# Chunk attention, then a top-1 cosine router with eight experts: two first weight loads issued from GpSimd, and three sums of the second stream computed by GpSimd

## The chip, the core and the metric

The kernel runs on one core of one Trainium2 chip. The metric is the device time of one execution in microseconds; the time of a kernel is the median of its runs. The profile shows one execution, with times counted from the start of its span. The engines are PE (TensorE: matmuls; "PEld" is its weight load), DVE (VectorE), ACT (ScalarE), POOL (GpSimd) and SP (SyncE, which here only issues DMAs). "SPq" and "POOLq" are the sequencers of SP and POOL, that is, their queues of instructions.

## The reference, cut to what matters

```python
# attention in chunks of 64: q, k, v are (8, 8, 576, 64)
scores = scale * (q_c @ k_c^T); attn = softmax(scores); out = attn @ v_c
x = out as (4608, 512)                                  # B*S rows, H*D columns
# router: one expert of 8 for each row
logits = normalise(x) @ normalise(expert_emb).T / tau
expert_idx = argmax(logits); gate_w = softmax(logits)[expert_idx]
for e in range(8):                                      # w1[e]: 512x1024, w2[e]: 1024x512
    h = maximum(x[mask_e] @ w1[e], 0)
    out[mask_e] = gate_w[mask_e] * (h @ w2[e])
```

Everything is float32. Which rows go to which expert is known only at run time.

## The kernel before, in words

**Two phases.** The first phase (to about 175 us of the span) computes the attention in 36 tiles of 128 rows, and the logits. It scatters each row into a DRAM buffer `spots`, where the rows of one expert lie together, in groups of 64 (`G`). At its end VectorE works out which group is computed in which step: `src_row` (where a group's rows lie), `eblk` (its expert), `fresh` and `swap` (whether other weights are needed than before), `after` and `more_e` (the next expert, and whether there is one). These are small integer tiles; the queues read them into registers.

The second phase is a row of steps. Each step `j` computes 128 rows: a group of 64 of stream 0, which walks up from expert 0, and a group of 64 of stream 1, which walks down from expert 7. So two sets of weights are in use at any time, `w1_sb[s]` and `w2_sb[s][buf]`, `s` = 0 or 1, each tile 2 MB. In the profile all of `w1_sb` and `w2_sb` read as `w`, and `next_w1` reads as `next_w`.

**What a step does.** `hidden_fast` (L323) computes `relu(x @ w1)` by Strassen's scheme in the form of Winograd: seven products of half the size instead of eight. Their order on PE is p1 (block B11 of w1), p2 (B21), p3 (B22), p5 (T1), p6 (T2), p7 (T3), p4 (T4). T1 to T4 are differences of blocks of w1. T1, T2 and T4 lie in `sums_sb[s]`; T3 overwrites B12 in w1 itself. Each product goes over both streams. `add_up` (L278, the instruction on L286) forms T1 to T4 by subtractions of 128x1024 elements on VectorE. `add_x` (L313) forms the sums S of the input, `turn_xb` (L198) turns the input's blocks. `result(j)` (L400) is the product with w2 (L408), scaling by the gate on ACT (L420) into the one buffer `y`, and a scatter to the output issued by POOL (L427). `y` has one buffer, so L420 of the next step waits until the scatter has read it.

Steps 0, 1 and 2 are computed without Strassen (`hidden_part`, L232); 0 and 1 still inside the first phase. The first Strassen step is step 3. Before it, VectorE must have formed T1, T2, T4 and T3 of both streams from the first weights (experts 0 and 7). The loop (L1146) writes, for `j` = 0: `add_up` of stream 0 between two pieces of the gates, then `result(0)`; for `j` = 1: `turn_next` (turn the input of step 3, issue the load of step 6, `add_x`), `add_up` of stream 1, the hidden part of step 2, and behind each of its halves T3 of that stream; then `result(1)`; from `j` = 2 on: `hidden_fast(j + 1)`, `result(j)`.

**Where the loads stand.** All loads of weights go through SP's queue (`load_when`, L169), in program order with the loads of rows (`load_x`, L158: four transfers `xin` on L148 and two `spot` on L154). A weight load is issued with a condition: its transfer takes place only where the flag is 1, but the instructions are always there: read the expert and the flag into registers (L132), then the DMA (L172). Ahead of the loop stand `load_x(4)`, `load_x(5)` and `load_w2(LONE)`, with `LONE` = 5: the second buffers of w2, first used by step 5, always loaded. In the loop, after `result(j)`, come `load_w2(next_of(j))` where that is 4 or more, and `load_behind(n)` (n = j + 2), which loads the next expert's w1 into `next_w1[s]`: `load_behind(3)` at j = 1 always loads, the later ones only where the expert before has been taken over. `load_w2(4)` stands after `result(3)`; it writes the buffers that results 0 to 4 read, and its flag is 0 where step 4 uses the same experts.

The order on each queue is the order of the program (a manual schedule); an engine waits at an instruction until the semaphores of what it needs have come. Where the expert changes, `take_next` (L290) copies three blocks by POOL (L296) while VectorE forms the sums.

Of the kernel before, what the change touches and what calls it, by code (L numbers as in the profile page):

```python
# [16 lines left out]
ENG = mybir.EngineType  # L17
# [8 lines left out]
def kernel(  # L26
# [11 lines left out]
    nc = tc.nc  # L38
    B, H, S, Dh = q.shape
    E, D = moe_expert_emb.shape  # L40
# [13 lines left out]
    NE = 4  # L54
# [6 lines left out]
    LONE = NE + 1  # L61

    def buf_of(j):
        return 0 if j < LONE else (j - LONE + 1) % 2
# [29 lines left out]
    w2_sb = [[keep.tile([P, KF, D], FP32, name=f"w2_{s}0")] for s in range(2)]  # L94
# [4 lines left out]
    w1_rows = moe_w1.rearrange("e (p c) f -> p e (c f)", c=KD)  # L99
    w2_rows = moe_w2.rearrange("e (p c) d -> p e (c d)", c=KF)  # L100
# [3 lines left out]
    eblk = keep.tile([P, NST], I32, name="eblk")  # L104
    fresh = keep.tile([P, NST], I32, name="fresh")
# [3 lines left out]
    after = keep.tile([P, NSW], I32, name="after")  # L109
    more_e = keep.tile([P, NSW], I32, name="more_e")  # L110

    def of_step(s, j):
        c = NST - 1 - (j - NE)
        return slice(G * s, G * s + 1), slice(c, c + 1)
# [6 lines left out]
    def whole(w):  # L121
        return w.rearrange("p c f -> p (c f)").unsqueeze(1)
# [8 lines left out]
    def number(ap, top, *engines):  # L131
        return nc.values_load(  # L132
            ap,
            engines=engines,
            min_val=0,
            max_val=top,
            skip_runtime_bounds_check_because="a count of comparisons, less than this",
        )
# [27 lines left out]
        r0 = (0, E - 1)[s] * R + G * j  # L166
        return spots[r0 : r0 + G * n, :]

    def load_when(w, rows, e, f):  # L169

        e, f = number(e, E - 1, ENG.SP), number(f, 1, ENG.SP)
        nc.sync.dma_start(  # L172
            out=whole(w), in_=rows[:, ds(e, 1), :], cond=f > 0, max_dma_last_dim=4096
        )

    def load_w2(j):
        for s in range(2):
            at = of_step(s, j)
            load_when(w2_sb[s][buf_of(j)], w2_rows, eblk[at], fresh[at])

    def load_behind(j):

        c = LEAST - 2 - j
        for s in range(2):
            at = (slice(G * s, G * s + 1), slice(c, c + 1))
            load_when(next_w1[s], w1_rows, after[at], more_e[at])

    def load_late(j):
        for s in range(2 if j != LEAST else 1):
# [79 lines left out]
    TS = ("T1", "T2", "T4")  # L269

    def block(s, m, w1=None):

        if m in TS:
            return sums_sb[s][:, TS.index(m)]
        u, v = UV[m]
        return (w1 or w1_sb)[s].rearrange("p (u c) (v x) -> p u v c x", u=2, v=2)[:, u, v]

    def add_up(s, w1, which):  # L278
        for o, a, b in (
            ("T1", "B12", "B11"),  # L280
            ("T2", "B22", "T1"),
            ("T3", "B22", "B12"),
            ("T4", "T2", "B21"),
        ):
            if o in which:
                nc.vector.tensor_tensor(  # L286
                    block(s, o), block(s, a, w1), block(s, b, w1), ALU.subtract
                )

# [155 lines left out]
    with (  # L445
# [43 lines left out]
        at = one.tile([P, 1], FP32, name="at")  # L489
# [551 lines left out]
        w = 2  # L1041
        for t in range(-1, 30):
            n = 2 if t in (8, 10, 24, 25) else 1
# [76 lines left out]
    next_w1 = [late_p.tile([P, KD, F], FP32, name=f"next_w1_{s}") for s in range(2)]  # L1120
    sums_sb = [late_p.tile([P, 3, KD // 2, F // 2], FP32, name=f"sums_{s}") for s in range(2)]

    load_x(NE)
    load_x(NE + 1)
    load_w2(LONE)

    with (
        tc.tile_pool(name="ps_h", bufs=1, space=PSUM, reuse_waits="tile") as ps_h,
        tc.tile_pool(name="ps_y", bufs=2, space=PSUM, reuse_waits="tile") as ps_y,
    ):  # L1130
        H_PS = [P, G // Q, KF * Q]

        def hidden_plain(j, w1, behind_it=None):
            for s in range(2 if j != LEAST else 1):
                ps = bank(ps_h, H_PS)
                for b in range(G // Q):
                    hidden_part(j, s, b, w1, None, None, ps)
                if behind_it is not None:
                    behind_it(s)

        def first_parts():
            for g in first_gates:
                next(g, None)

        first_parts()
        for j in range(LEAST - 1):  # L1146
            n = j + 2

            def turn_next():
                if n < LEAST:  # L1150
                    turn_xb(n)
                    if n + XBUF < NJ:
                        load_x(n + XBUF)
                    add_x(n)

            def swap_next():
                if NE <= n < LEAST:
                    take_next(n)

            if j == 0:  # L1160
                first_parts()
                add_up(0, None, TS)
                first_parts()
            elif j == 1:
                turn_next()
                add_up(1, None, TS)
                hidden_plain(2, w1_sb, lambda s: add_up(s, None, ("T3",)))
            else:
                gate = gate_parts(n) if n < LEAST else iter(())
                hidden_fast(j + 1, ps_h, gate, turn_next, swap_next)  # L1170

            result(j, ps_y)
            if NE <= next_of(j) < NJ:
                load_w2(next_of(j))
            if NE - 1 <= n < LEAST - 1:
                load_behind(n)
            elif n == LEAST - 1:
                load_late(LEAST)

        steps = number(n_steps, NST, ENG.PE, ENG.DVE, ENG.Activation, ENG.Pool, ENG.SP)  # L1180

        odd_one = number(n_odd, 1, ENG.PE, ENG.DVE, ENG.Activation, ENG.Pool, ENG.SP)

        def before_last():
            result(LEAST - 1, ps_y)
            load_w2(LEAST + 1)

        def step_alone(j, between=None):
            turn_xb(j)
            if j + XBUF < NJ:  # L1190
                load_x(j + XBUF)
            gates(j)
            hidden_plain(j, next_w1)
            if j + 1 < NJ:
                load_late(j + 1)
            if between is not None:
                between()
            result(j, ps_y)
            if j + 2 < NJ:
                load_w2(j + 2)  # L1200

        def more(j):
            if j == NJ:
                return

            with tc.If(steps > j - NE - 1):  # L1206
                step_alone(j)
                more(j + 1)

        had, had_mo, had_gate = dict(xin), dict(mo), dict(gate_of)  # L1210
        with tc.If(odd_one > 0) as if_odd:  # L1211
            step_alone(LEAST, before_last)
            more(LEAST + 1)
        for now, then in ((xin, had), (mo, had_mo), (gate_of, had_gate)):
            now.clear()
            now.update(then)
        with if_odd.Else():
            del xin[LEAST]
            load_x(LEAST + XBUF)
            before_last()  # L1220
            load_w2(LEAST + 2)
            load_late(LEAST + 1)
            more(LEAST + 1)
# [28 lines left out]
```

## Time and profile before

| | |
|---|---|
| time, median of 3 runs | 659.24 us (655.4 to 660.79) |
| the profiled execution: its time / its span | 657.75 us / 656.0 us |
| PE busy | 617.0 us (94%) |
| DVE / ACT / POOL busy | 425.3 us (65%) / 429.7 us (66%) / 183.9 us (28%) |
| largest group: L408, product with w2 | 278.0 us |
| the seven Strassen products on L337 (1056 + 1056 + 1056 + 528 instructions) | 108.4 + 109.0 + 82.3 + 53.4 us |
| DMA queue of SP (q1) / of POOL (q0) | 71.99 MB / 38.89 MB |

A line of the page's groups reads: line, engine, operation, output <- input, count, busy time, mean, and the idle time of the engine ahead of it with what ended it. The timeline gives the start, the duration, the engine and, in brackets, how long the engine had idled and what released it. The table of windows gives for each stretch the busy time of PE, PEld, DVE, ACT and POOL with counts, then the granted clock of PE (1.00 is full speed), the busy share of the DMA engines and their GB/s. From about 236 us to 645 us PE is busy almost without a gap, one step in 12.91 us.

### The profile page before, as it was taken

To read this page: it belongs to the slowest core of one execution; us is meant where nothing else is said; L and a number is where in the kernel's file an instruction comes from. 1 tells how busy PE (TensorE), PEld (TensorE's weight loads), DVE (VectorE), ACT (ScalarE), POOL (GpSimd) and SP (SyncE) were. 2 spreads that over 40 slices of the span, in tenths; PEclk is the share of its full clock that TensorE was granted. 3 is DMA by queue.
4 is the path that set the end of the run, shared out by engine and by line. 5 is a ranking of instruction groups with operands and counts; after the bars stand their busy time and mean duration, and the time that the engine had idled before them with its cause. 6 is when DMAs were issued, how large, how long until landed. Compare 5 with 4: busy or idle time off the path is not lost. (4 is left out here: it accounts for less than half of the span.)

```text
span 656.0 us, 24867 instructions
## 1 busy us (share of the span) xinstructions
PE 617.0 (94%) x9744; PEld 344.5 (53%) x9744; DVE 425.3 (65%) x1140; ACT 429.7 (66%) x758; POOL 183.9 (28%) x262
## 2 busy tenths in 40 slices
PE   6899989898898989999999999999999999999993
PEld 5778878775443435445444544665444444444431
DVE  4878888786697446647784566979546666654430
ACT  4767767674316757767676767776777777676650
POOL 7759897762410100003020002303010021000101
PEclk9999999999998999999999999999999999999998
DMA  9999999988528711112787111776821116311111
GB/s 259 302 253 276 275 293 283 333 280 299 220 64 304 285 41 40 46 39 72 285 316 265 53 44 43 292 302 236 341 62 44 47 39 217 129 39 35 51 32 36
DMA packets 91696, 112.68 MB, mean 172 GB/s; under 512 B 49260, under 2 KB 69484, under 8 KB 91560
## 3 DMA queue, kind: packets, MB, share of 16 engines
q1 hardware_dynamic: 79512, 71.99, 34.0%
q0 software_dynamic: 12016, 38.89, 17.5%
q8 instruction: 81, 1.33, 0.8%
q14 instruction: 55, 0.45, 0.2%
q10 hardware_dynamic: 32, 0.02, 0.0%
HBM read 334.71 MB, written 22.69 MB: 545 GB/s over the span
## 5 line engine op out<-in xcount | busy, mean ns | idle before, releaser
L408 PE MATMUL y_ps<-w,hT 128*32 128x512 f32 (+1 forms) x2368 | 278.0, 587 | 2.9 <-DMA w<-in_moe_w_dram 2.9
L356 ACT ACTIVATE h<-C 64x256 f32<-64x256 f32 x264 | 179.4, 679 | 69.9 <-DVE C L369 67.1
L408 PEld LDWEIGHTS y_ps<-w,hT 128*32 128x32 f32 x2368 | 91.2, 110 | 155.4 <-issue 136.0
L427 POOL DMA_INDIRECT out_dram<-y,spot x36 | 37.5, 1042 | 392.4 <-ACT y L420 301.6
L337 PE MATMUL h<-w,S 128*32 128x256 f32 x1056 | 108.4, 382 | 1.8 <-DVE w L286 1.8
L337 PE MATMUL h<-sums,xbT 128*32 128x256 f32 x1056 | 109.0, 383 | 0.5 <-DVEq L294 0.5
L369 DVE TENSOR_TENSOR C<-C,h 128x256 f32<-128x256 f32 x231 | 96.0, 416 | 11.2 <-PE h L337 4.4
L363 DVE STREAM_TRANSPOSE hT<-h 128x512 f32<-128x512 f32 x66 | 46.7, 708 | 55.2 <-ACT h L356 54.5
L337 PE MATMUL h<-w,xbT 128*32 128x256 f32 x1056 | 82.3, 379 | 0.0
L222 DVE TENSOR_SCALAR rn<-rn 128x1 f32<-128x1 f32 x37 | 5.6, 151 | 87.6 <-ACT rn L219 87.6
L337 PEld LDWEIGHTS h<-w,S 128*32 128x32 f32 x1056 | 49.3, 110 | 24.2 <-DVE w L286 1.5
L337 PEld LDWEIGHTS h<-sums,xbT 128*32 128x32 f32 x1056 | 49.4, 111 | 23.2 <-DVEq L294 1.4
L337 PEld LDWEIGHTS h<-w,xbT 128*32 128x32 f32 x1056 | 43.6, 110 | 31.6 <-issue 9.0
L420 ACT ACTIVATE y<-y_ps,gate 128x512 f32<-128x512 f32 x36 | 24.8, 688 | 50.6 <-issue 44.7
L337 PE MATMUL h<-sums,S 128*32 128x256 f32 x528 | 53.4, 379 | 0.0
L816 POOL DMA_INDIRECT spots<-xr,dest x36 | 37.4, 1039 | 28.0 <-DVE dest L781 9.8
L198 DVE STREAM_TRANSPOSE xbT<-xin 128x256 f32<-128x256 f32 x73 | 44.4, 646 | 0.5 <-DVE hT L363 0.5
L219 ACT ACT_TABLE_LOAD x34 | 43.6, 1283 | 0.9 <-issue 0.4
L226 ACT ACT_TABLE_LOAD x34 | 43.6, 1283 | 0.6
L698 ACT COPY xT<-tr 128x512 f32<-128x512 f32 x36 | 21.1, 586 | 32.3 <-PE tr L696 32.3
L586 POOL DMA_DIRECT2D kx<-in_k_dram x36 | 31.9, 888 | 13.4 <-PE tr L612 12.6
L586 POOL DMA_DIRECT2D qx<-in_q_dram x40 | 34.5, 865 | 0.7 <-PE tr L612 0.6
(204 smaller groups left out, 802.2 us busy)
## 6 DMA issues: line engine op xcount, KB each, us to landing
w<-in_moe_w_dram SPq DMA_DIRECT2D x74, 2048.0 KB
next_w<-in_moe_w_dram SPq DMA_DIRECT2D x67, 2048.0 KB
xin<-spots SPq DMA_DIRECT2D x158, 64.0 KB
qx<-in_q_dram POOLq DMA_DIRECT2D x32, 256.0 KB, 5.9
v<-in_v_dram SPq DMA_DIRECT2D x58, 128.0 KB
kx<-in_k_dram POOLq DMA_DIRECT2D x28, 256.0 KB, 4.6
spots<-blank SPq DMA_DIRECT2D x9, 144.0 KB
spot<-spots SPq DMA_DIRECT2D x80, 4.0 KB
```

The source lines that it names most:

```text
L198: nc.vector.transpose(xT[:, :, cols].rearrange("p c (b i) -> p b c i", i=Q), t[:, s * (D // 2) : (s + 1) * (D // 2)].rearrange("p (b i c) ...
L219: nc.scalar.activation(rn, spot[:, j % SPOTS, SQ : SQ + 1], AF.Sqrt)
L226: nc.scalar.activation(sh, sh, AF.Exp, accum_out=gate)
L337: nc.tensor.matmul(ps[t0 : t0 + Q], lhsT=a[:, c, s], rhs=w[:, r], start=c == 0, stop=c == KD // 2 - 1,)
L356: nc.scalar.activation(h[b][G * v : G * v + G, s].rearrange("p (k i) -> p k i", i=Q), x[G * s : G * s + G].rearrange("p (i k) -> p k i", i=Q),
L363: nc.vector.transpose(hT.rearrange("p k (s b i) -> p b s k i", b=2, i=Q)[:, b], h[b].rearrange("p s (k i) -> p s k i", i=Q),)
L369: nc.vector.tensor_tensor(out, a, b, op)
L408: nc.tensor.matmul(ps[Q * r : Q * r + Q, 0:w], lhsT=d["hT"][:, c, Q * t0 : Q * t0 + Q], rhs=w2_sb[s][buf_of(j)][:, c, d0 : d0 + w], start= ...
L420: nc.scalar.activation(y[:, 0:w], ps[:, 0:w], AF.Copy, scale=gate_of.pop(j))
L427: ins = nc.gpsimd.indirect_dma_start(out=to, out_offset=bass.IndirectOffsetOnAxis(ap=at, axis=0), in_=y[:, 0:w], in_offset=None, bounds_ch ...
L586: eng.dma_start(out=x[done : done + n], in_=src[b, :, s : s + n, :].rearrange("h p d -> p h d"),)
L816: ins = nc.gpsimd.indirect_dma_start(out=spots, out_offset=bass.IndirectOffsetOnAxis(ap=at, axis=0), in_=m, in_offset=None, bounds_check=S ...
```

## The change

Three things are moved; nothing is added or left out of the computation.

1. `load_w2(5)`, ahead of the loop, is issued by POOL instead of SP: two transfers of 2 MB.
2. `load_behind(3)`, after `result(1)`, is issued by POOL instead of SP: two transfers of 2 MB. All later weight loads stay on SP.
3. T1, T2 and T4 of stream 1 from the first weights are formed by POOL instead of VectorE, and the call stands one step earlier in the program, at `j` = 0 beside that of stream 0. T3 of both streams stays on VectorE. The later sums, in `take_next`, stay where they were.

The order of instructions on POOL is then: the last scatters of the first phase, the two loads of `load_w2(5)`, T1, T2, T4, the scatter of `result(0)`, the scatter of `result(1)`, the two loads of `load_behind(3)`, and on as before. VectorE loses three instructions, SP loses four transfers and their register reads; PE and ACT keep theirs.

```diff
-    def load_when(w, rows, e, f):
+    def load_when(w, rows, e, f, by=(nc.sync, ENG.SP)):
 
-        e, f = number(e, E - 1, ENG.SP), number(f, 1, ENG.SP)
-        nc.sync.dma_start(
+        e, f = number(e, E - 1, by[1]), number(f, 1, by[1])
+        by[0].dma_start(
             out=whole(w), in_=rows[:, ds(e, 1), :], cond=f > 0, max_dma_last_dim=4096
         )
...
+    BY_POOL = (nc.gpsimd, ENG.Pool)
...
-    def add_up(s, w1, which):
+    def add_up(s, w1, which, eng=nc.vector):
...
             if o in which:
-                nc.vector.tensor_tensor(
+                eng.tensor_tensor(
                     block(s, o), block(s, a, w1), block(s, b, w1), ALU.subtract
                 )
...
     load_x(NE)
     load_x(NE + 1)
-    load_w2(LONE)
+    load_w2(LONE, BY_POOL)
...
             if j == 0:
                 first_parts()
                 add_up(0, None, TS)
+                add_up(1, None, TS, nc.gpsimd)
                 first_parts()
             elif j == 1:
                 turn_next()
-                add_up(1, None, TS)
                 hidden_plain(2, w1_sb, lambda s: add_up(s, None, ("T3",)))
...
             if NE - 1 <= n < LEAST - 1:
-                load_behind(n)
+                load_behind(n, *([BY_POOL] if n == NE - 1 else []))
```

(`load_w2` and `load_behind` hand `by` on to `load_when`.)

More of the change, by code (lines that the diff above doesn't have):

```diff
@@ L167, in first_rows, with load_w2, load_behind @@
         return spots[r0 : r0 + G * n, :]
-    def load_when(w, rows, e, f):
-        e, f = number(e, E - 1, ENG.SP), number(f, 1, ENG.SP)
-        nc.sync.dma_start(
+    def load_when(w, rows, e, f, by=(nc.sync, ENG.SP)):
+        e, f = number(e, E - 1, by[1]), number(f, 1, by[1])
+        by[0].dma_start(
             out=whole(w), in_=rows[:, ds(e, 1), :], cond=f > 0, max_dma_last_dim=4096
         )
-    def load_w2(j):
+    BY_POOL = (nc.gpsimd, ENG.Pool)
+    def load_w2(j, *by):
         for s in range(2):
             at = of_step(s, j)
-            load_when(w2_sb[s][buf_of(j)], w2_rows, eblk[at], fresh[at])
-    def load_behind(j):
+            load_when(w2_sb[s][buf_of(j)], w2_rows, eblk[at], fresh[at], *by)
+    def load_behind(j, *by):
         c = LEAST - 2 - j
@@ L185, in load_behind @@
             at = (slice(G * s, G * s + 1), slice(c, c + 1))
-            load_when(next_w1[s], w1_rows, after[at], more_e[at])
+            load_when(next_w1[s], w1_rows, after[at], more_e[at], *by)
     def load_late(j):
```

## The prediction, made before the changed kernel was run

> **What bounds the kernel now.** I read the page first: PE is busy for 617.0 of 656.0 us, so only a place where PE stands or runs slowly can be won. Where does it? The timeline, reduced to the first product p1 of each Strassen step, gives the starts 195.71, 212.55, 225.46, 242.07 and 255.00 us. The intervals are 16.84, 12.91, 16.61 and 12.93 us; from there on a step takes 12.91 us to the end. So two steps are too long, by 3.93 and by 3.70 us. Both lie where the change acts. The waits between 170 and 250 us name them (total us, times, longest):
>
> ```profile
> PE y_ps L408 <- DMA w<-in_moe_w_dram: 2.9, 2, 2.6
> PE h L337 <- DVE w L286: 1.8, 2, 1.0
> ```
>
> The first place: p7 of step 3 waits for T3, which VectorE forms last. The timeline shows the chain on VectorE: T1 of stream 0, the turned input, T4 of stream 1 behind it, T3 of stream 1 at the end.
>
> ```profile
> 188.19 1.22 DVE L286 TENSOR_TENSOR sums<-w 128x1024 f32<-128x1024 f32 x1
> ...
> 192.88 1.23 DVE L198 STREAM_TRANSPOSE xbT<-xin 128x256 f32<-128x256 f32 x2
> ...
> 197.90 1.23 DVE L286 TENSOR_TENSOR sums<-sums,w 128x1024 f32<-128x1024 f32 x1
> ...
> 201.40 1.21 DVE L286 TENSOR_TENSOR w<-w 128x1024 f32<-128x1024 f32 x1
> ```
>
> The table of windows shows the rest of that loss: after the two waits the granted clock (third column from the right) is halved for some 3.4 us, which costs 1.7 us.
>
> ```profile
> 203.00:204.00 1.00, 1.00 (x16) 0.55 (x12) 0.93 (x5) 1.00 (x1) 0.00 (x0) 0.50 1.07 397
> 204.00:205.00 1.00, 1.00 (x16) 0.52 (x12) 0.98 (x2) 0.99 (x4) 0.00 (x0) 0.50 0.99 324
> 234.00:235.00 1.00, 0.29 (x2) 0.14 (x4) 0.86 (x3) 0.96 (x3) 0.00 (x0) 1.00 0.06 15
> ```
>
> The second place: `result(4)` waits for `load_w2(4)`, which transfers nothing, but whose instruction SP reaches only at 234.60. SP is late:
>
> ```profile
> 194.97 2.03 SPq L172 DMA_DIRECT2D w<-in_moe_w_dram  x2
> ...
> 199.87 4.88 SPq L154 DMA_DIRECT2D spot<-spots  x1
> ...
> 225.64 1.40 SPq L172 DMA_DIRECT2D next_w<-in_moe_w_dram  x2
> ...
> 234.60 1.40 SPq L172 DMA_DIRECT2D w<-in_moe_w_dram  x2
> ```
>
> A `spot` issue takes 0.51 us as a rule (80 issues, minimum 0.510, median 0.515); behind the 2 MB loads it takes 4.88 here and 5.20 us at 215.22. At 232 us the clock stays at 1.00.
>
> **SP's part: a gain of 3.7 us.** The change takes off SP two pairs of loads. With their register reads they stand from 193.45 (end of the `spot` before) to 197.00, and from about 208.9 (register read of `after`) to 212.4: 3.5 + 3.4 = 6.9 us of issue. The long `spot` issues (4.88, 2.30, 5.20, 1.96 us at 199.87 to 222.18) come on top. PE was free for `result(4)` at 232.1; the first instruction of `load_w2(4)` would stand at 234.6 - 6.9 = 227.7 even if the long issues stayed, and the second 1.3 us behind. So the wait vanishes: -3.70 us, the whole excess of that step. What can put it back: `load_behind(4)`, still on SP and ahead of `load_w2(4)`, writes `next_w1` again and must wait until POOL's transfers have landed. From its register reads (about 224.2) to `load_w2(4)` SP takes 10.4 us. POOL issues `load_behind(3)` after the scatter of `result(1)`, by my sum at about 207; before, such a pair was issued at 210.4 and the DMA engines fell quiet at about 224, 13.5 us later. Landed at 220.5, then 9 to 10 us: `load_w2(4)` at 230, needed at 233. That is a margin of 3 us; the bound without it is a gain of 0.
>
> **POOL's part: the start.** POOL is free after the last scatter of the first phase at 181.3. It must wait for `eblk` and `fresh`, which VectorE writes until 183.31 and 184.04. A register read on POOL takes 0.47 us (64 reads of `swap`), other registers 0.2, a plain load's issue 0.87 us (qx, 40 issues). So the first load is issued at about 185, the second until 187.7, and T1 begins at about 187.8.
>
> **POOL's part: the time of one sum.** The trace has no subtraction of 128x1024 elements on POOL. From below: a copy of that size takes 1.04 us (18 copies on L296). From above: its small TENSOR_TENSORs take 0.204 us for 8 columns (L552) and 0.273 and 0.302 us for 41 (L543, L542), so 2.1 to 3.0 ns a column, and 2.3 to 3.2 us for 1024. I take 2.3, the lower slope, which is nearer to the copy. VectorE takes 1.22.
>
> The Trainium skill, GPSIMD Engine Reference, section "Elementwise — side-by-side cycle accounting", speaks against this part: two-input arithmetic is about half as fast there (4497 ns against 2293 for 2048 elements), and VectorE stays the engine for it. Halved, an estimate from that page, a sum would take 2.25 us; in the sum below that gives the same result within 0.2 us.
>
> **POOL's part: whom it holds up.** That POOL is slower would cost nothing, since T1 of stream 1 is needed by p5 at 198.3. But VectorE forms the sums of stream 0 from 188.19 to 191.93, at the same time, and the trace shows that the two don't run together. In this stretch three copies run on POOL, and VectorE's two-input L313 beside them:
>
> ```profile
> 414.95 3.06 POOL L296 COPY w<-next_w 128x1024 f32<-128x1024 f32 x3 [1.09 <-DVE C L369]
> 416.01 1.11 DVE L313 TENSOR_TENSOR S<-xbT 128x128 f32<-128x128 f32 x1
> 417.15 1.01 DVE L313 TENSOR_TENSOR xbT<-xbT 128x128 f32<-128x128 f32 x1
> 418.19 0.29 DVE L313 TENSOR_TENSOR S<-xbT 128x128 f32<-128x128 f32 x1
> ```
>
> L313 takes 0.29 us alone and 1.11 and 1.01 beside a copy: it ends when the copy ends. At 445 to 450 us copies and L286 take turns in the same way (L286 1.76 and 1.94 us instead of 1.22, one copy 2.03). The transposes (L198: 1.24 instead of 1.21) and sums with one operand in PSUM (L369) are not held. So VectorE's T1, T2, T4 of stream 0 alternate with POOL's: VectorE is held two to nearly three times, 4.6 to 6.5 us with 2.3 us each; I take 5.5. Call it D.
>
> **What D does.** VectorE's chain behind these sums is gates, turned input, `add_x`, transposes and T3. Input turned: 194.1 + D = 199.6. `add_x` done: 195.47 + D. From there no sums of stream 1 stand before the first transpose, and the stretch from it to the end of T3 takes 3.57 us (199.04 to 202.61): T3 is done at 199.04 + D = 204.5, against 202.61 before. Removing 3.7 us from VectorE while holding it for 5.5 makes T3 later. PE is free at 195.9 and now waits for the input until 199.6, where it did not wait before. Behind T3 it needs 12 of 16 instructions of p7, p4 and `result(2)`: 0.65 + 0.86 + 6.87 (218.59 to 225.46) = about 8.3 us: the next p1 at 212.9, if the clock stays. If the wait of 3.7 us halves the clock for the 3 us that follow, p1 to p6 (5 x 0.86) take until 205.5, and the next p1 comes at 205.5 + 8.6 = 214.1. Of the two idle places in this trace one halved it and one didn't; I take the middle, 213.5, +1.0 us against 212.55. Bounds: at 1.04 us a sum, D is 2.4, p1 comes at 199.04 + 2.4 + 8.3 = 209.7, -2.8; at 3.2 us D is up to 8, T3 ends at 207.0, p1 comes at 215.3 to 216.9, +2.8 to +4.4. Sums done before VectorE needs the port, or no turns taken, would give the whole 3.93.
>
> **Moves that cost nothing.** The loads of step 5's w2 start at 185 instead of 195; nothing reads them before 246. The scatter of `result(0)` now stands behind T4 and, on POOL's DMA queue, behind 4 MB: these are through at about 199, 13.5 us after 185. ACT's L420 of `result(1)` waits for that scatter to have read `y`; the gates of `result(0)` move by D, so it is issued at about 199.5 and lands 2.8 us (median) to 4.5 later, at 203. ACT then copies p1 by 204.6, and p4, which writes the same bank, comes at 206. That cover is 1.5 us; beyond it each us is a us of PE.
>
> **The sum.** -3.7 + 1.0 = -2.7 us. On the profiled execution: 657.75 - 2.7 = 655.0 (span 653.3). That execution lies 1.5 us below the median, and the change goes with the step starts, so 659.24 - 2.7 = 656.5 us.
>
> **Rivals.** *Both stalls go* (chance 0.20): POOL's sums and VectorE's don't collide, because POOL's come out shorter or at other moments. For it: T1 on POOL needs no VectorE at all, and VectorE is rid of 3.7 us. Against: the turns above. 659.24 - 3.93 - 3.70 = 651.6. *The late load stays* (0.13): `load_behind(4)` holds SP until POOL's load has landed. For it: the wait is there, with 3 us of margin. Against: POOL issues it earlier than SP did. 659.24 + 1.0 = 660.2. *GpSimd holds VectorE longer than SP's part brings* (0.17), the slower side: place 188 to 205 us, price D - 5.2 us (199.04 + D + 8.3 against 212.55) and up to 1.6 of halved clock; it decides from D = 8.9, or 7.4 with the clock halved. For it: the upper slope (3.2 us a sum) gives D = 8. Against: the lower. At D = 8 with the clock halved +4.4 - 3.7: 659.9; a sum of 5 us would be needed for 1%.
>
> **How the numbers follow.** The forecast has 0.50, its own range is 653.5 to 659.5 (the +0.4 and +1.6 of the clock, and a spread of runs of some 2.5 us to each side). The wider range, 651.0 to 662.0, takes in both stalls gone and the late load with the spread. About 1%, 6.6 us, is what a measurement of this kernel can tell from no change; faster by that needs nearly all of the 7.6 us: 0.20, the first rival. Slower by it: 0.10, the far half of the last. The rest, 0.70, is within.
>
> **What would show it.** Right: POOL's L286 line (now L289) with three sums of 2 us or more, VectorE's beside them 3 us long instead of 1.22; p1 of step 3 waiting for L198 (now unseen) by 3 to 4 us; no wait of L408 for `w`, and SP's issue of `load_w2(4)` before 232; the intervals of p1 about 17 to 18, 12.9, 12.9. Wrong: sums of VectorE at 1.22 throughout, or an interval near 12.9 in the first place (both stalls gone), or L408 still waiting at 232.

## The result, and the profile after

The changed kernel takes 660.74 us (median; 657.71 to 663.39), the kernel before, on the same chip, 656.33 us: ratio 1.0063, 95% interval [1.0036, 1.009]. It is slower by some 4.1 us. On three other chips, shown below, the ratio was 1.0034 [1.0013, 1.0056], 1.0046 [1.0018, 1.0073] and 1.0015 [0.998, 1.005]; the last can't be told from no change. The profiled execution took 662.32 us, its span 660.7 us. Lines behind the diff are three higher than before: L286 is now L289, L296 is L299, L313 is L316, L337 is L340, L408 is L411; L297 is the conditional block of a take-over.

First the waits of PE between 170 and 260 us. Both waits of before (L408 for `w`, L337 for T3) are gone, and a larger one is there:

```profile
PE h L340 <- ACT h L261: 4.6, 1, 4.6
```

It stands ahead of p1 of step 3, at 195.88 to 200.49 us. What ends there is named as ACT; at the same moment VectorE delivers the turned input, and in the profiles of 6, 7, 11, 13 and 15 the same wait is put down to that (`xbT`). Why that is late is seen in POOL's timeline, then in VectorE's:

```profile
181.20 0.82 POOL L172 DMA_DIRECT2D w<-in_moe_w_dram  x1
...
183.13 2.40 POOL L289 TENSOR_TENSOR sums<-w 128x1024 f32<-128x1024 f32 x1
185.60 2.38 POOL L289 TENSOR_TENSOR sums<-w,sums 128x1024 f32<-128x1024 f32 x1
188.07 2.40 POOL L289 TENSOR_TENSOR sums<-sums,w 128x1024 f32<-128x1024 f32 x1
```

```profile
182.84 2.74 DVE L930 TENSOR_SCALAR src_row<-row 128x39 int32<-128x39 f32 x1
...
185.70 2.33 DVE L933 CAST eblk<-e_of 128x39 int32<-128x39 f32 x1
...
188.15 2.35 DVE L953 TENSOR_SCALAR swap<-e_of 128x9 int32<-128x9 f32 x1
...
195.03 1.22 DVE L289 TENSOR_TENSOR sums<-w 128x1024 f32<-128x1024 f32 x1
...
199.72 1.15 DVE L201 STREAM_TRANSPOSE xbT<-xin 128x256 f32<-128x256 f32 x2
```

POOL's three sums lie end to end, and under each one lies a small instruction of VectorE of 39 or 9 columns. In the profile of before the same three take 0.18, 0.18 and 0.23 us:

```profile
182.83 0.18 DVE L927 TENSOR_SCALAR src_row<-row 128x39 int32<-128x39 f32 x1
...
183.13 0.18 DVE L930 CAST eblk<-e_of 128x39 int32<-128x39 f32 x1
...
183.44 0.23 DVE L950 TENSOR_SCALAR swap<-e_of 128x9 int32<-128x9 f32 x1
```

VectorE's own first sum starts at 195.03 instead of 188.19: 6.84 us late. PE, starved for 4.6 us, then runs at half clock (third column from the right) from 200.5 to about 205.6:

```profile
201.00:202.00 1.00, 1.00 (x14) 0.53 (x14) 0.90 (x4) 0.00 (x0) 0.16 (x1) 0.50 0.26 100
...
204.00:205.00 1.00, 1.00 (x16) 0.52 (x12) 1.00 (x2) 0.19 (x1) 0.00 (x0) 0.50 0.23 57
```

So p1 of step 4 comes at 216.01 instead of 212.55 us, 3.46 later. The second place is mended: SP reaches `load_w2(4)` at 229.85 instead of 234.60, and steps 4 to 7 follow at 12.91 us each.

```profile
212.97 6.13 SPq L154 DMA_DIRECT2D spot<-spots  x1
...
229.85 1.35 SPq L172 DMA_DIRECT2D w<-in_moe_w_dram  x2
```

At step 7 the kernels stand level: p1 at 254.75, before 255.00. The whole loss comes later, in the stretch that the prediction took for unchanged: from p1 of step 7 to the last scatter it takes 395.97 us, before 390.82. 4.50 of these 5.15 us fall in one step, from 332.20 to 349.62 us (17.41 us instead of 12.91), behind the take-over of new weights at 326 us. POOL's copies begin while VectorE forms the sums on the input; three of these four, 0.29 us each alone, are held:

```profile
326.47 3.13 POOL L299 COPY w<-next_w 128x1024 f32<-128x1024 f32 x3 [3.35 <-DMA next_w<-in_moe_w_dram]
```

```profile
326.23 0.29 DVE L316 TENSOR_TENSOR S<-xbT 128x128 f32<-128x128 f32 x1
326.55 1.10 DVE L316 TENSOR_TENSOR xbT<-xbT 128x128 f32<-128x128 f32 x1
327.68 1.01 DVE L316 TENSOR_TENSOR S<-xbT 128x128 f32<-128x128 f32 x1
328.73 1.01 DVE L316 TENSOR_TENSOR S<-xbT,S 128x128 f32<-128x128 f32 x1
```

VectorE's take-over sums then start at 333.14 us. PE waits 2.60 us for them and again runs at half clock, to about 342 us:

```profile
338.01 0.84 PE L340 MATMUL h<-sums,xbT 128*32 128x256 f32 x10 [2.60 <-DVEq L297]
```

In the profile of before the copies start at 327.40, just behind the last input sum, which ends at 326.86:

```profile
326.57 0.29 DVE L313 TENSOR_TENSOR S<-xbT,S 128x128 f32<-128x128 f32 x1
...
327.40 3.00 POOL L296 COPY w<-next_w 128x1024 f32<-128x1024 f32 x3 [4.83 <-DMA next_w<-in_moe_w_dram]
```

The rest is lost in two later steps with a take-over: 0.3 us in the one that starts at 453.10 us, 0.36 in the one at 544.67. Three take-overs also have VectorE's first sum wait longer (at 306.56, 427.98 and 543.32 us; only the last of them is followed by a longer step of PE). Two of them, in the profile after:

```profile
306.56 1.23 DVE L289 TENSOR_TENSOR sums<-next_w 128x1024 f32<-128x1024 f32 x1 [1.30 <-issue]
...
543.32 1.22 DVE L289 TENSOR_TENSOR sums<-next_w 128x1024 f32<-128x1024 f32 x1 [0.34 <-issue]
```

In before the corresponding waits are 0.87 us and none; at the take-over between them it is 1.25 us instead of 0.88.

```profile
306.45 1.23 DVE L286 TENSOR_TENSOR sums<-next_w 128x1024 f32<-128x1024 f32 x1 [0.87 <-DVEq L294]
```

### The profile page after: what moved, and what is told of

Same layout as the page of the kernel before. It is cut to its first block, busy times and chain, and to the rows that moved or that the text cites. A ratio compares the mean times of both kernels' runs of the same rounds, so it can differ in the third digit from the quotient of the medians.

```text
span 660.7 us, 24875 instructions
## 1 busy us (share of the span) xinstructions
PE 620.0 (94%) x9744; PEld 352.5 (53%) x9744; DVE 435.0 (66%) x1137; ACT 429.7 (65%) x758; POOL 196.1 (30%) x269
## 5 line engine op out<-in xcount | busy, mean ns | idle before, releaser
L411 PE MATMUL y_ps<-w,hT 128*32 128x512 f32 (+1 forms) x2368 | 269.1, 586 | 0.0
L411 PEld LDWEIGHTS y_ps<-w,hT 128*32 128x32 f32 x2368 | 100.8, 110 | 142.5 <-issue 101.6
L340 PE MATMUL h<-sums,xbT 128*32 128x256 f32 x1056 | 93.4, 381 | 3.5 <-DVEq L297 3.5
L340 PE MATMUL h<-w,S 128*32 128x256 f32 x1056 | 94.0, 386 | 0.0
L340 PE MATMUL h<-w,xbT 128*32 128x256 f32 x1056 | 76.6, 387 | 4.7 <-ACT h L261 4.6
L340 PEld LDWEIGHTS h<-w,xbT 128*32 128x32 f32 x1056 | 41.9, 112 | 36.9 <-issue 7.1
L340 PEld LDWEIGHTS h<-sums,xbT 128*32 128x32 f32 x1056 | 46.1, 111 | 28.2 <-DVEq L297 5.4
L340 PEld LDWEIGHTS h<-w,S 128*32 128x32 f32 x1056 | 46.8, 112 | 23.7 <-issue 1.7
L201 DVE STREAM_TRANSPOSE xbT<-xin 128x256 f32<-128x256 f32 x73 | 48.0, 696 | 0.5 <-DVE hT L366 0.5
L340 PE MATMUL h<-sums,S 128*32 128x256 f32 x528 | 46.9, 385 | 0.0
```

The costliest lines, as they stand in the source:

```text
L201: nc.vector.transpose(xT[:, :, cols].rearrange("p c (b i) -> p b c i", i=Q), t[:, s * (D // 2) : (s + 1) * (D // 2)].rearrange("p (b i c) ...
L340: nc.tensor.matmul(ps[t0 : t0 + Q], lhsT=a[:, c, s], rhs=w[:, r], start=c == 0, stop=c == KD // 2 - 1,)
L411: nc.tensor.matmul(ps[Q * r : Q * r + Q, 0:w], lhsT=d["hT"][:, c, Q * t0 : Q * t0 + Q], rhs=w2_sb[s][buf_of(j)][:, c, d0 : d0 + w], start= ...
```

## The experiments

All times "from the first memset" count from POOL's memset on L90 that opens the expert stage (181.12 us of the span before, 181.13 after): the first phase ahead of it differs by some us between executions. On two chips (the first four and the last three kernels here) PE itself comes to step 3 some 5 us or more later, with gaps ahead of single matmuls that are put down to "issue" (from PE's last wait in the first phase to p1 of step 3 the kernel before takes 29.2 us there instead of 24.1). What these gaps are is open. There VectorE's chain is not the first thing that delays PE, and these profiles say little about the first place.

**1. The loads alone** (`load_w2(LONE, BY_POOL)` and `load_behind` as in the change, the sums left on VectorE) and **2. the sums alone**. Both come once more as 10 and 11, on a chip where PE has no gaps of its own.

```diff
# 1: without
-                add_up(1, None, TS, nc.gpsimd)
# 2: without
-    load_w2(LONE, BY_POOL)
+    load_w2(LONE)
```

> Only the four loads go to POOL; all sums stay on VectorE. Theory H (POOL's sums hold VectorE's small instructions for 6.8 us and cost 3.5 us at the first place; the loads off SP give 3.7 us at the second; the other 4 us of the changed kernel's loss are a later collision of POOL's copies with add_x): first interval of p1 16.8 us as before, second 12.9 instead of 16.6, so 3.7 us faster than before, ratio 0.994, if the take-over near 326 us does not collide; with it about equal. Rival Q (2 MB loads on POOL's queue are what costs, in the steps after 255 us): not faster than before, ratio 1.000 or more, with L408 or L420 waiting for DMAs.

> Only the three sums go to POOL; all loads stay on SP. H: POOL's sums start at about 181.3 us, at once after the scatters, and hold three of VectorE's small instructions for 2.2 to 2.6 us each; p1 of step 3 starts at about 200.5 instead of 195.7, first interval of step starts 20 us counted from 195.7. load_w2(4) is late by less, since PE is now late itself: second interval 12.9 to 14. In sum 0 to 4 us slower than before, ratio 1.000 to 1.006. Rival Q: the sums are harmless for the total, ratio below 1.002. A third reading, that POOL's descriptor writing for 2 MB loads is what held VectorE: VectorE's small instructions at 0.2 us here.

Measured: loads 0.9968 [0.994, 0.9997], sums 1.0037 [1.0005, 1.007]. With the sums alone VectorE is held too, twice here (POOL's first sum ran while VectorE waited for ACT):

```profile
197.24 2.34 DVE L913 TENSOR_SCALAR grp<-grp,step,off 128x39 f32<-128x39 f32 x1
...
200.13 2.88 DVE L920 TENSOR_TENSOR pr<-ge,jump 128x624 f32<-128x624 f32 x1
```

With the loads alone these two take 0.30 and 0.81 us, nothing is held in this stretch, and VectorE's sums take 1.22 us. So the sums hold VectorE, and POOL's loads do not.

**3. The changed kernel and 4. the kernel before, once more**, for their profiles on that chip.

> The changed kernel once more, for its profile. H: VectorE held for 6.8 us again at 183 to 190 us, the first interval about 20.3 counted from 195.7, the next ones 12.91; at the take-over of the second stream near 326 us POOL's copies and add_x collide again or not: if they do, 660 to 663 us, if not, 656 to 658. Rival Q: 660 or more with no such collision.

> The kernel before once more, for its profile. H: intervals 16.8, 12.9, 16.6, 12.9 at the start of the steps again; from 255 us on the same steps but for the take-overs, where collisions of POOL's copies with add_x may come and go: that is what runs of 653.6 to 660.8 us differ by. Rival Q: take-overs as in the first profile, within 0.5 us.

Measured: 668.51 and 664.19 us, one execution each. The three holds came again (2.10, 2.40, 2.85 us, on L905, L913 and L920). At the second take-over one input sum was held, and PE waited 0.30 us instead of 2.60. The late load of the kernel before cost 1.40 us there instead of 3.70 (an interval of 14.31 us instead of 12.91).

**5. Loads by POOL, all sums on VectorE, T4 of stream 1 behind T3.**

```diff
             if j == 0:
                 add_up(0, None, TS)
-                add_up(1, None, TS, nc.gpsimd)
             elif j == 1:
                 turn_next()
+                add_up(1, None, ("T1", "T2"))
                 hidden_plain(2, w1_sb, lambda s: add_up(s, None, ("T3",)))
+                add_up(1, None, ("T4",))
```

> The loads go through GpSimd's queue as in the change, all sums stay on VectorE, and T4 of stream 1 is formed behind T3 of stream 1 instead of ahead of the input transposes. In the run with the loads alone T3 of stream 1 ended at 212.98 us and p4 could begin some 0.65 us later. Theory (the place is set by VectorE's chain in front of T3, and the sums need not be moved to another engine): T3 ends 1.2 us earlier, T4 takes its old place, p4 begins when T4 is there: 0.6 us less up to p1 of step 4 than with the loads alone, so 32.8 us from the first memset of the expert stage instead of 33.45, no wait of result(4) for w, ratio to the kernel before 0.995 to 0.998. Rival (PE stops in p4 instead and its clock halves, or the order makes nothing of it): p1 of step 4 at 33.4 or later, ratio 0.997 to 1.000.

Measured: 0.9861 [0.9832, 0.989], far better than both kernels. p1 of step 4 comes 28.77 us from the first memset: 2.66 less than in the kernel before, where I had expected 0.6 less than with the loads alone. That expectation rested on a profile in which PE's own gaps hid the place. T3 of stream 1 ends at 20.25 us from the memset instead of 21.49, PE waits 0.80 us once instead of 0.80 and 1.03, and the clock stays at 1.00. The second place is not quite mended, for PE is now there before the load: the interval is 14.45 us, 1.54 too long.

```profile
228.60 1.05 PE L411 MATMUL y_ps<-w,hT 128*32 128x512 f32 x4 [0.50 <-DMA w<-in_moe_w_dram]
```

**6. GpSimd's sums in pieces of 256 columns.**

```diff
+                k = 128 if eng is nc.gpsimd else F // 2
+                for i in range(0, F // 2, k):
                     eng.tensor_tensor(
-                    block(s, o), block(s, a, w1), block(s, b, w1), ALU.subtract
+                        block(s, o)[:, :, i : i + k], ..., ALU.subtract
```

> The changed kernel, but each of GpSimd's three sums is issued as four of 128x256 elements. Theory (whenever GpSimd has a sum to run, VectorE's next instruction with both operands in SBUF waits to its end, so that VectorE loses what GpSimd uses, in whatever portions): twelve holds of some 0.7 us in place of three of 2.4, VectorE's own sums start 6 to 9 us later than without the holds (6.84 us in the changed kernel), p1 of step 4 at 34.5 to 37 us from the first memset. Rival (a hold is what remains of the one instruction in flight, and VectorE gets through several small ones in between): holds of 0.3 to 0.7 us, fewer than ten of them, VectorE's sums 3 us late or less, p1 of step 4 at 31 to 32.5 us, 2 us better than the changed kernel.

Measured: 1.0072 [1.0046, 1.0098]; p1 of step 4 at 35.79 us. The total is that of the theory, the form is that of neither. POOL's timeline and VectorE's:

```profile
184.04 2.80 POOL L291 TENSOR_TENSOR sums<-w 128x256 f32<-128x256 f32 x4
186.81 2.80 POOL L291 TENSOR_TENSOR sums<-w,sums 128x256 f32<-128x256 f32 x4
189.57 2.79 POOL L291 TENSOR_TENSOR sums<-sums,w 128x256 f32<-128x256 f32 x4
```

```profile
183.76 8.65 DVE L935 TENSOR_SCALAR src_row<-row 128x39 int32<-128x39 f32 x1
```

One instruction of 39 columns stands through all twelve pieces. Between POOL's whole sums (0.07 us apart in the changed kernel) the held instruction ends and one or two more get through; between the pieces, which follow each other without a gap, none does. Cutting the work small makes the hold longer (8.47 us instead of 6.84).

**7. Three spare instructions on VectorE**, to test whether the longer wait in the take-overs comes from where the conditional blocks lie in VectorE's program.

```diff
+                if j == 2:
+                    spare = bp.tile([P, 1], FP32, tag="spare", name="spare", bufs=1)
+                    for _ in range(3):
+                        nc.vector.memset(spare, 0.0)
```

> The changed kernel with three spare memsets of 128x1 on VectorE in step 4, so that VectorE's program has as many instructions ahead of its conditional blocks as the kernel before; they cost less than 0.2 us of VectorE off the path. Theory (the 0.4 us more at each take-over of new weights comes from where the conditional block lies in VectorE's program, with three instructions fewer ahead of it): VectorE's first sum of a take-over waits 0.86 to 0.88 us instead of 1.26 to 1.30, and the two late take-over steps take 13.04 and 13.08 us instead of 13.46 and 13.43. Rival (it is the neighbourhood of GpSimd's sums or their dependences): 1.26 to 1.30, 13.46 and 13.43 again.

Measured: the waits were 1.24 and 1.32 us, the steps, read as intervals between the scatters of `result`, 13.52 and 13.37. So the theory fell as it was put. That the place plays no part is not shown by it: at the last take-over the wait was 0.13 us instead of 0.34. (The added tile did something else, told at the end: the first phase took 23.5 us longer.)

**8. The changed kernel, timed on that chip.**

> The changed kernel once more, timed, with another profile. Theory (the 4.1 us of the first profile at 326 us, where GpSimd's three take-over copies met VectorE's sums on the inputs, is a matter of where SP's queue happens to be, and comes in some runs only; what always stays is some 2.5 us more at the first place, 1.8 to 3.7 less at the second, 0.8 at the take-overs): ratio 1.000 to 1.005, and a profile in which the copies cost less than 1 us. Rival (the collision belongs to the change): the copies cost 4 us again, ratio 1.006 or more.

Measured: 1.0034 [1.0013, 1.0056]; its profile is the lowest of its twelve executions, with one input sum held and a wait of 0.49 us. So the collision differs from execution to execution.

**9. Wait once for GpSimd.** Because POOL has written T1, T2 and T4 of stream 1, VectorE's first two sums of each later conditional take-over of stream 1 carry one wait more, for POOL. The trace shows these instructions in VectorE's queue, two in each of the two take-overs of stream 1 (the first two of the six stand ahead of the sums of stream 0 and T3, the last at 429.2 us):

```profile
L289 DVEq EVENT_SEMAPHORE  x6: 21/21/50, 194.8 to 429.2; - x6
```

One small read of T4 outside of the conditional blocks makes them superfluous.

```diff
+                if j == 2:
+                    spare = bp.tile([P, 1], FP32, tag="spare", name="spare", bufs=1)
+                    nc.vector.tensor_copy(spare, sums_sb[1][:, 2, 0, 0:1])
```

> The changed kernel with one more small copy on VectorE in step 4, which reads one element of T4 of stream 1. After it VectorE has waited for GpSimd's three sums once, and the waits for GpSimd that the changed kernel has in front of the first two sums of every conditional take-over of stream 1 fall away. Theory (the 0.35 to 0.44 us more at each take-over of stream 1 is these waits, which GpSimd's writing of the sums brings into every later block): VectorE's first sum of such a take-over waits 0.87 us or nothing, as in the kernel before, the late take-over steps take 13.04 and 13.08 us, and the time is 0.8 us under the changed kernel's. Rival (it is not the waits, since three spare instructions did not mend it either): 1.26 to 1.30 and 0.34 again, 13.46 and 13.43. The hold at 183 to 190 us and the collision at the take-over copies are untouched: p1 of step 4 at 34 to 35 us from the first memset, ratio 1.000 to 1.004.

Measured: the waits are back at 0.86 us and none, the two intervals of the scatters at 13.14 each, no such instruction is left in the take-overs, and no input sum was held at the second take-over. So the added instructions bring the longer waits about. That VectorE stands in them is not so: each takes 0.02 us (the median above). In the changed kernel the time lies between other entries of VectorE's queue: 0.44 us instead of 0.08 ahead of the register read at 305.79, 0.46 instead of 0.15 behind the branch at 426.6, and 0.42 instead of 0.05 behind the branch at 542.84, in a take-over of stream 0 that carries no added wait. How the added instructions cause this is open. Nor does all of it cost PE time: the first of the two intervals is made up by a shorter next one (11.65 us instead of 12.44), and by the starts of p1 only the last of the three take-overs comes with a longer step, 13.44 us against 13.08. The time of this run (1.0331) says nothing, since the first phase again took 21 us longer.

**10 and 11. The loads alone, the sums alone, once more; 12. T4 behind T3 alone**, with the loads on SP (the edit of 5 on the kernel before).

> Only the loads of the change, as in the first run of them, beside the next three on one chip. Theory (SP's part brings 3.7 us at the second place and nothing is lost elsewhere, the rest is GpSimd's sums): ratio 0.992 to 0.996, the interval behind step 6's first product 12.91 us, first place as in the kernel before (T3 waited for 1.8 us in two parts, where PE has no gaps of its own). Rival (SP's part brings less, the late load returns in most runs): 0.996 to 1.000.

> Only the sums of the change. Theory (the first place costs 2.5 to 3.5 us more, the take-overs 0.8, the meeting of copies and input sums up to 4.1 in some runs): ratio 1.005 to 1.011, p1 of step 4 some 34 to 35 us from the first memset. Rival (the sums cost only the small loss that the first run of them showed): 1.001 to 1.005.

> The kernel before with one line moved: T4 of stream 1 is formed behind T3 of stream 1, on VectorE; the loads stay on SP. Theory (VectorE's chain in front of T3 is what bounds the first place, and 1.2 us less of it lets PE run through): p1 of step 4 at 28.8 us from the first memset instead of 31.4, ratio 0.994 to 0.997, and the late load of step 4 stays: it costs as much or more, since PE is there earlier. Rival (the 0.986 of loads and moved T4 together came from the order alone): 0.986 to 0.990.

| kernel | p1 of step 4 | last scatter | ratio |
|---|---|---|---|
| before | 31.43 | 464.70 | |
| loads alone (10) | 29.75 | 459.34 | 0.9943 [0.9914, 0.9973] |
| sums alone (11) | 34.79 | 465.04 | 0.9989 [0.9963, 1.0015] |
| T4 behind T3 alone (12) | 28.75 | 465.07 | 0.9988 [0.9958, 1.0017] |
| loads, T4 behind T3 (5) | 28.77 | 460.35 | 0.9861 [0.9832, 0.989] |
| the change (first; 8) | 34.88; 33.95 | 469.59; 464.63 | 1.0063; 1.0034 |

(us from the first memset in the profile; the ratio is that of the timed runs, each beside the kernel before on its chip.) This is the table that explains the case. The loads alone gain 5.36 us in the profile: 3.70 at the second place, and 1.68 at the first, where PE waits for T3 as long as in the kernel before but keeps its clock this time; why it does is not shown. The sums alone lose 3.36 us at the first place and yet nothing in sum on this chip (on the chip of 2 they cost 0.4%). The reason is in SP's rows: it reaches `load_w2(4)` at 233.05 us, and PE, itself 3.4 us late, now needs it no sooner; the interval at the second place is 12.91 us.

```profile
233.05 1.40 SPq L172 DMA_DIRECT2D w<-in_moe_w_dram  x2
```

Moving T4 alone is the mirror image. PE is early, the load is not, and what was won is waited away (5.09 us, and 1.7 more by the half clock that follows):

```profile
231.37 8.71 PE L408 MATMUL y_ps<-w,hT 128*32 128x512 f32 x62 [5.09 <-DMA w<-in_moe_w_dram]
```

The late load is thus a deadline that SP sets. Bringing it forward is worth 3.7 us only to a PE that arrives on time; a PE that the sums have made late has no use for it. In the changed kernel one part removes a wait that the other part has already made void.

**13 to 15.** As 9, with the spare tile 32 elements wide; as 5; the changed kernel.

> The changed kernel with the one small copy on VectorE in step 4 that reads T4 of stream 1, its tile now 128 bytes a partition instead of 4. Theory (the waits for GpSimd in the take-overs cost 0.4 us each and, by that delay, bring the take-over copies and VectorE's sums on the inputs together; a tile of 4 bytes shifted addresses and so slowed the first phase): first memset of the expert stage at 180 to 182 us instead of 202, none of the sums on the inputs held at the second take-over, no wait of PE there, 3 to 4 us under the changed kernel on the same chip, ratio to the kernel before 0.996 to 1.000. Rival (the collision comes whether or not the waits are there): within 1 us of the changed kernel, ratio 1.002 to 1.006. If the first phase is slow again, it is not the tile's size.

> Loads by GpSimd, all sums on VectorE, T4 of stream 1 behind T3, as in the fifth experiment. Theory (2.7 us at the first place, 3.7 at the second): 6.4 us, ratio 0.988 to 0.992, p1 of step 4 at 28.8 us from the first memset. Rival (the 0.986 was a lucky set of five runs, or the late load comes back, as its profile showed 0.7 us of it): 0.992 to 0.995.

> The changed kernel, beside the two above on one chip. Theory (the collision at the second take-over comes in most of its runs): ratio 1.003 to 1.007, the profile with one or three held sums there. Rival (the earlier ratios were the chips'): 0.999 to 1.002 and no held sum.

Measured: 1.0167 [1.0133, 1.0201] with a first phase 13 us longer; 0.9899 [0.9862, 0.9937]; 1.0046 [1.0018, 1.0073]. The waits were 0.87 us and none in the first, with no input sum held and 464.33 us to the last scatter; in the changed kernel 1.28 and 0.35, two sums held, PE waiting 1.20 us, 466.87 us. The version of 5 again has the lowest ratio: 1.0% to 1.4% under the kernel before. How much of that is the moved T4 is not shown. Its two profiles reach the last scatter at 460.35 and 460.06 us, no sooner than the loads alone (459.34), since the late load costs PE 1.5 us in both; but these two executions are 2.2 and 3.5 us above the median of their runs, and the loads alone were timed on other chips.

**16. Wait once, without a new tile; 17. T1 alone on POOL; 18. the changed kernel.**

```diff
# 16
+                if j == 2:
+                    nc.vector.tensor_copy(sums_sb[1][:, 2, 0, 0:1], sums_sb[1][:, 2, 0, 0:1])
# 17
-                add_up(1, None, TS, nc.gpsimd)
+                add_up(1, None, ("T1",), nc.gpsimd)
...
                 turn_next()
+                add_up(1, None, ("T2", "T4"))
```

> The changed kernel; in step 4 VectorE copies one element a partition of T4 of stream 1 onto itself, so that it has waited for GpSimd's sums once; no tile is added. Theory (the added waits cost 0.4 us at each take-over of stream 1 and make GpSimd's copies meet VectorE's input sums at the second take-over): first memset at 180 to 182 us, no wait of PE at the second take-over, 464.3 to 465 us from the first memset to the last scatter (changed kernel: 469.59, 464.63 and 466.87), ratio to the kernel before 0.997 to 1.001, some 3 us under the changed kernel on the same chip. Rival (the waits are worth 0.8 us and the collision comes as often): 1 us under it, ratio 1.002 to 1.005.

> Both loads and T1 of stream 1 alone moved to GpSimd; T2 and T4 stay on VectorE. Theory (VectorE waits once for each sum on GpSimd, some 2.3 us, and saves 1.22 us): its sums of stream 0 start 2.2 to 2.5 us later than with the loads alone, T3 of stream 1 ends 1.1 us later, p1 of step 4 at 30.5 to 31.5 us from the first memset (29.75 with the loads alone, 34 to 35 with all three sums), ratio 0.995 to 0.998. Rival (a loss only from several sums in a row): 29.0 to 29.8, ratio 0.992 to 0.995.

> The changed kernel beside the two above. Both theories: ratio 1.003 to 1.006, one to three input sums held at the second take-over.

Measured: 0.9997 [0.9971, 1.0022], 0.999 [0.9962, 1.0019], 1.0015 [0.998, 1.005]. This was the second chip on which PE has gaps of its own, and the first place could not be read: 17 stays undecided. The take-overs could. VectorE's timeline in 16:

```profile
316.38 1.23 DVE L289 TENSOR_TENSOR sums<-next_w 128x1024 f32<-128x1024 f32 x1 [0.85 <-DVEq L297]
...
547.77 1.23 DVE L289 TENSOR_TENSOR sums<-next_w 128x1024 f32<-128x1024 f32 x1
```

The waits are gone, no input sum is held, and from the memset to the last scatter it takes 465.68 us, against 467.06 in 18 with one sum held. By the medians 16 is 1.1 us faster than 18, nearer to the rival's 1 than to the theory's 3; the intervals of the two overlap.

## Why the prediction was wrong

**The tally.** Up to the last scatter the profile after is 4.9 us behind that of before, where 2.7 us less were forecast. Of these 7.6 us, 2.45 belong to the first place (+3.46 instead of +1.0) and 5.15 to the stretch behind step 7, which the step "The sum" put at nothing ("the change goes with the step starts"). SP's term was right in this profile.

**The place and the size of the hold (the step "POOL's part: the start").** This step failed first. It let POOL wait for `eblk` and `fresh` until 183.31 and 184.04 us. Step 5 needs only the columns that VectorE had written at 177.66 to 177.9, in an earlier, smaller round of the same function. So the first load was issued at 181.20, not at 185, and T1 began at 183.13, not at 187.8. The sums therefore met not VectorE's three sums of stream 0 but the small instructions ahead of them, and nearly the whole time of POOL's three sums (7.18 us) was lost to VectorE. D was 6.84 us instead of 5.5. The time of one sum was right (2.38 to 2.40 against 2.3).

**What D does.** The formula held: T3 was to end at 199.04 + 6.84 = 205.9, and ended at 205.68. But T3 was not last. PE started at 200.49 and was at half clock for 5.1 us, where the prediction had allowed for 3, so p7 began only at 207.44. The term of +1.0 us measured +3.46, and +2.5 to +3.8 in the other two profiles of the changed kernel where PE has no gaps. The prediction's choice of "the middle" between a halved and a full clock was the weak point: a wait of 4.6 us was followed by the half clock in each of these three, for 5.1, 3.4 and 6.1 us. With D at 6.84 and the clock halved the prediction's own price, D - 5.2 and 1.6, gives +3.2.

**SP's part.** Right in this profile, -3.70 us, although the `spot` issue at 212.97 took 6.13 us; `load_w2(4)` came at 229.85 where 230 was forecast. What the text did not see is that it is no gain to be added to any first place: the sums alone remove the same wait (experiment 11). With the first place at +3.46 the sum at step 7 is -0.25; and with SP's part left out altogether the last scatter comes no more than 0.34 us behind that of the kernel before.

**What was not in the sum.** The forecast took everything behind step 7 for unchanged. The profiles of the changed kernel lose 5.15, 1.13 and 2.13 us there. Two causes. The added waits for POOL lengthen VectorE's wait at three take-overs by 0.34 to 0.43 us; that they bring it about is shown by 9, 13 and 16, which take them away. By PE's steps they are worth some 0.36 us, at the last take-over; the 0.3 us at 453.10 are not theirs, since that step takes 14.00 to 14.16 us in 9, 13 and 16 as well (14.11 after, 13.80 before). The larger cause is the collision, 4.50, 0.73 and 1.42 us of PE's steps in the three. The collision of POOL's copies with VectorE's input sums at the second take-over stands in the seven profiles that have both parts of the change and the added waits (one to three sums held, PE waiting 0.30 to 2.60 us). It stands in none of the others, neither with one part alone nor with the waits removed. How near the two lie shows in the starts, counted from p1 of step 12: in the seven the input sums begin at 6.14 to 6.93 us and the copies at 6.48 to 7.17; in the two of the kernel before it is 6.05 and 7.22 to 7.86, with the loads alone 5.64 to 5.74 and 7.33 to 7.35, with the sums alone 5.97 and 7.11 to 7.15, without the added waits 5.61 to 6.39 and 7.29 to 7.69. So some tenths of a us on either side decide. That the waits and the earlier SP together bring it about is what this pattern suggests; the timed test of it (16 against 18) left 1.1 us, on a chip where the collision was small, so its full share is not shown. No rival had named it: the prediction had this collision on the page (414.95 us) and used it only as evidence for another place.

**The rivals.** The nearest was *GpSimd holds VectorE longer*. Its price was right in kind; its point of decision, D of 7.4 with the clock halved, was just missed by 6.84 with a longer half clock. That put the two places at level, and the take-overs decided.

## What to carry to other kernels

When work is moved to an engine that holds the relieved one up while it runs, as GpSimd held VectorE here (6.84 us for 7.18 us of sums), count the mover's whole time as a loss of the other from the moment at which it can start, and look up which columns or bytes it really waits for. Two stalls on one path are not two gains: ask of each whether it is a delay or a deadline, and test the parts alone, since here one part gained 0.3% to 0.6%, the other cost nothing or 0.4%, and both together cost between 0.15%, which is not told from nothing, and 0.6%. Reordering the sums on the same engine, together with the moved loads, gave 1.0% to 1.4% without moving any arithmetic. And ask what the moved work does to the rest of the program: in the profile after the larger part of the error lay in steps that the change does not touch.

## What the runs showed of the hardware that was not expected

- **A hold lasts as long as GpSimd leaves no gap.** An instruction of 0.18 us was held 8.65 us over twelve sums of GpSimd. The Trainium skill, SBUF — State Buffer, section "Who interferes with whom", says that of two such instructions the later waits until the earlier one has ended; the 2.3 to 2.7 us holds agree, the 8.65 us is longer than any single instruction there (0.7 us).
- **A writer on another engine costs at later conditional blocks.** Three sums on GpSimd at 183 us put four semaphore waits of 0.02 us into VectorE's later take-overs, and its wait in three take-overs, up to 360 us later, grew by 0.34 to 0.43 us. One read by VectorE outside of the blocks took away both. The time stands beside the branches and not in the waits; why is open.
- **A small tile in the wrong pool.** In all three kernels with a new tile in `bp` (4 bytes a partition in 7 and 9, 128 in 13) the first phase was 13 to 24 us longer. In 13 a large piece of that lies at 15 to 20 us, where PE stands idle, waiting for `kx`. The table of windows shows it, first for 13 (last numbers: busy share of the DMA engines, GB/s):

```profile
15.00:20.00 5.00, 0.00 (x0) 0.00 (x0) 0.00 (x0) 0.67 (x2) 0.00 (x0) 0.66 1.09 217
```

and for the changed kernel on the same chip (15):

```profile
15.00:20.00 5.00, 4.95 (x120) 4.27 (x119) 4.14 (x9) 3.19 (x6) 3.52 (x8) 1.00 1.14 325
```

The DMA engines are as busy and move a third less. That addresses behind the tile moved is likely; which of them matters was not tried.
